# Shifting the SBUF places of three weight slots and two activation pools, with a smaller DMA scratch

## Chip, cores and metric

One core of a Trainium2 chip runs the whole program. The metric is the time of one execution in microseconds on the device, the median of several runs. [...]

## What is computed

Linear attention with an exponential feature map, then two gated feed-forward layers on the same 2304 tokens, all in float32.

```python
# q, k, v: (4, 8, 576, 64), w_phi: (64, 128)
def phi(x):
    proj = np.einsum('bhsd,df->bhsf', x, w_phi)
    proj = proj - np.max(np.abs(proj), axis=-1, keepdims=True)
    return np.concatenate([np.exp(proj), np.exp(-proj)], axis=-1)
q_p, k_p = phi(q), phi(k)
kv = np.einsum('bhsf,bhsd->bhfd', k_p, v)
z = np.sum(k_p, axis=2)
attn = np.einsum('bhsf,bhfd->bhsd', q_p, kv) / (np.einsum('bhsf,bhf->bhs', q_p, z)[..., None] + 1e-06)
x = attn.transpose(0, 2, 1, 3).reshape(2304, 512)
# layer 1, then layer 2 the same with sigmoid(x @ w_gate) in place of silu(x @ w_gate)
x = (silu(x @ w_gate) * (x @ w_val)) @ w_out       # 512 -> 1536 -> 512
```

## The kernel before

**Stages.** The program begins with the attention (about the first 150 us of the span): small float32 matmuls on lines 688, 724, 751 and 787, beside which VectorE, ScalarE and GpSimd turn the packed weights into float32 (lines 522 to 554). Then come the two layers, each in two passes `hh` over half of the hidden columns (`hh` 0 and 1 are the first layer, 2 and 3 the second). A pass goes over five token blocks (`BLOCKS`: four of 512 tokens, one of 256) in the order `ROUTE[hh]`, and for each block over three pieces `p` of its weights (`NPAIR`). One (hh, block, p) is a unit.

**A unit.** Every float32 operand is split into a high and a low part in the type fp32r (`plan_halves`, lines 573 and 579: ScalarE casts the high part, VectorE subtracts for the low one), and a product is three matmuls, high by high, high by low, low by high. In a full unit the gate and value products are done with seven block products instead of eight (`PROD`); `product` on line 1024 issues them, each matmul with a weight tile of 128 x 128 as the stationary operand and 256 columns of x as the moving one. Each of the seven block products is 12 matmuls, so a full unit has 84 of them; a unit of the 256-token block has four block products, 48 matmuls. They write the PSUM banks `a` and `b`; ScalarE and VectorE combine them (lines 1044, 1050), apply the gate (1062), multiply (1067) and split the result into `uh` and `ul`. The second product of the unit, `accumulate`, is issued inside the next unit: 24 matmuls of 512 columns for a full unit. In passes 0 and 1 (line 1099) the weights `o` are stationary and `u` moves; in passes 2 and 3 (line 1101) `u` is stationary and `o` moves.

**Order.** It is written out: `ORDER` gives for a full unit 24 matmuls of `product`, 12 of `accumulate` ("a", "b"), 48 of `product`, 9 of `accumulate` ("c", "d0"), 12 of `product`, 3 of `accumulate` ("d1"). A table of times sorts all calls once, and each engine's instructions stand in that order. All data DMAs are issued from SyncE's queue.

**Places in SBUF.** A weight slot is the pool `w0`, `w1` or `w2` with the tiles `w{p}h`, `w{p}l`, `o{p}h`, `o{p}l`; piece p always uses slot p. The pools `x0` and `x1` hold `xh` and `xl`; blocks alternate between them: x0 has the first, third and fifth block of passes 0 and 1 and the second and fourth of passes 2 and 3, x1 has the others. Pool `u` holds `c0`, `c1`, `uh`, `ul`. The pool `stage` holds the pieces that DMAs load and store. Pools are stacked from the left or the right end of each partition; w2 and x1 are opened when the attention's own pools have been closed (`swap`). A weight slice of one matmul is 128 floats, 512 bytes in a partition; a slice of x is 1024 bytes and one of u or o as a moving operand 2048. So all slices of a tile begin at the same place modulo 512 as the tile itself.

Of the kernel before, what the change touches and what calls it, by code (L numbers as in the profile page):

```python
# [10 lines left out]
F32 = mybir.dt.float32  # L11
# [9 lines left out]
P = 128  # L21
# [12 lines left out]
LINE = 32  # L34
# [419 lines left out]
def body(ctx: ExitStack, tc: tile.TileContext, qT, kT, v, w_phi2, wpk, out):  # L454
    nc = tc.nc
# [7 lines left out]
            for k, side in enumerate(("left", "right"))]  # L463
    wides = [x.__enter__() for x in wide]
    pools = {w: ctx.enter_context(tc.tile_pool(name=w, bufs=1)) for w in ("w0", "w1")}
    stage = ctx.enter_context(tc.tile_pool(name="stage", bufs=1))
    pools["x0"] = ctx.enter_context(tc.tile_pool(name="x0", bufs=1))
    pools["u"] = ctx.enter_context(tc.tile_pool(name="u", bufs=1))

    xT = [dram.tile([KC, P, S], F32, name=f"xT{b}") for b in range(B)]  # L470
# [731 lines left out]
    def pool(name, side="left"):  # L1202
        return tc.tile_pool(name=name, bufs=1, side=side, reuse_waits="tile")

    edge = ctx.enter_context(pool("edge", "right"))
    edge.tile([P, 3 * LINE // 4], F32, name="edge")
    aq, ap, ak, ae = pool("aq"), *(pool(name, "right") for name in ("ap", "ak", "ae"))
    aq_, *ap_ = (x.__enter__() for x in (aq, ap, ak, ae))
    T0, ready = plan_attention(*ap_, aq_, 0.0)
# [1 line left out]
    def swap(old, side, *names):  # L1211
        for x in reversed(old):
            x.__exit__(None, None, None)
        for name in names:
            pools[name] = ctx.enter_context(pool(name, side))

    for k in range(2):
        at(ready["w"][1 - k], part_banks, k)
    at(ready["e"], swap, (ap, ak, ae), "right", "w2")
    at(ready["nd"], swap, (aq,), "left", "x1")  # L1220

    T0 += TS
# [85 lines left out]
```

## Time and profile before

| | us |
|---|---|
| median of 3 runs | 993.05 (992.68 to 998.37) |
| the profiled execution, its own time | 996.62 |
| its span, first to last instruction | 994.5 |
| PE busy in the span | 980.9 (99%) |
| VectorE, ScalarE, GpSimd busy | 692.4, 527.2, 38.8 |

The span is 2.1 us shorter than the profiled execution's own time, and that execution lies 3.6 us above the median. PE busy counts matmuls whose ends are modelled, so 99% says that PE always has a matmul under way, not how fast they follow each other; that is read from the starts of successive matmuls.

### The profile page before, as it was taken

To read this page: it belongs to the slowest core of one execution; us is meant where nothing else is said; L and a number is where in the kernel's file an instruction comes from. 1 tells how busy PE (TensorE), PEld (TensorE's weight loads), DVE (VectorE), ACT (ScalarE), POOL (GpSimd) and SP (SyncE) were. 2 spreads that over 40 slices of the span, in tenths; PEclk is the share of its full clock that TensorE was granted. 3 is DMA by queue.
4 is the path that set the end of the run, shared out by engine and by line. 5 is a ranking of instruction groups with operands and counts; after the bars stand their busy time and mean duration, and the time that the engine had idled before them with its cause. 6 is when DMAs were issued, how large, how long until landed. Compare 5 with 4: busy or idle time off the path is not lost.

```text
span 994.5 us, 20911 instructions
## 1 busy us (share of the span) xinstructions
PE 980.9 (99%) x8632; PEld 891.5 (90%) x8632; DVE 692.4 (70%) x1220; ACT 527.2 (53%) x977; POOL 38.8 (4%) x40
## 2 busy tenths in 40 slices
PE   7999999999999999999999999999999999999998
PEld 6777778999999999999999999999999999999997
DVE  6999888938757795368787897486677834555343
ACT  5988977535545564264454574455546534334321
POOL 1433210000000000000000000000000000000000
PEclk9999999999999999999999999999999999999999
DMA  7566876436535532066554442446416002132011
GB/s 239 167 216 211 262 240 197 149 126 182 196 118 153 183 96 83 1 198 213 155 174 134 167 156 77 141 141 197 144 70 191 23 21 86 64 128 86 1 44 42
DMA packets 67551, 136.00 MB, mean 137 GB/s; under 512 B 9408, under 2 KB 35712, under 8 KB 67456
## 3 DMA queue, kind: packets, MB, share of 16 engines
q1 hardware_dynamic: 67456, 134.68, 42.4%
q8 instruction: 67, 1.10, 0.4%
q14 instruction: 28, 0.23, 0.1%
HBM read 94.66 MB, written 39.99 MB: 135 GB/s over the span
## 4 chain that ended last, share of the span: by engine, by line
PE 95%; DVE 3%; DMA 1%; ACT 0%; issue 0%; SPq 0%; DVEq 0%; ACTq 0%
PE a L1024 30%; PE b L1024 23%; PE c L1101 8%; PE c L1099 8%; PE d L1099 8%; PE d L1101 6%; PE d L787 5%; PE c L724 3%; PE w L688 3%; DVE sub L697 1%; DVE m L695 1%; PE w L751 1%; DMA xT<-nd 1%; DMA x<-kT 0%; ACT eq L771 0%
## 5 line engine op out<-in xcount | busy, mean ns | idle before, releaser
L1050 DVE TENSOR_TENSOR c<-b,c 128x512 f32<-128x512 f32 x96 | 66.0, 687 | 118.9 <-PE b L1024 109.9
L1062 ACT ACTIVATE c<-c 128x256 f32<-128x256 f32 x96 | 50.3, 525 | 147.0 <-DVE c L1050 147.0
L1044 ACT COPY c<-a 128x512 f32<-128x512 f32 x96 | 56.4, 587 | 111.9 <-PE a L1024 109.3
L573 DVE TENSOR_TENSOR ul<-c,uh 128x512 fp32r<-128x512 f32 (+1 forms) x120 | 75.8, 635 | 33.3 <-ACT uh L579 32.5
L579 ACT CAST uh<-c 128x512 fp32r<-128x512 f32 (+1 forms) x120 | 69.3, 580 | 41.6 <-DVE c L1067 33.3
L1024 PE MATMUL a<-xh,w0h 128*128 128x256 f32 x288 | 80.7, 280 | 0.0
L1024 PE MATMUL a<-xh,w1h 128*128 128x256 f32 x288 | 80.5, 280 | 0.0
L1024 PE MATMUL a<-xh,w2h 128*128 128x256 f32 x288 | 80.5, 279 | 0.0
L1024 PE MATMUL a<-xl,w0h 128*128 128x256 f32 x288 | 80.3, 279 | 0.0
L1024 PE MATMUL a<-xl,w2h 128*128 128x256 f32 x288 | 80.3, 279 | 0.0
L1024 PE MATMUL a<-xl,w1h 128*128 128x256 f32 x288 | 80.3, 279 | 0.0
L1024 PE MATMUL a<-xh,w0l 128*128 128x256 f32 x288 | 80.2, 279 | 0.0
L1024 PE MATMUL a<-xh,w2l 128*128 128x256 f32 x288 | 80.2, 279 | 0.0
L1024 PE MATMUL a<-xh,w1l 128*128 128x256 f32 x288 | 80.2, 278 | 0.0
L1067 DVE TENSOR_TENSOR c<-c 128x256 f32<-128x256 f32 (+1 forms) x96 | 52.9, 555 | 29.4 <-ACT c L1062 29.4
L1024 PE MATMUL b<-xh,w0h 128*128 128x256 f32 x224 | 62.5, 279 | 0.0
L1024 PE MATMUL b<-xh,w0l 128*128 128x256 f32 x224 | 62.4, 279 | 0.0
L1024 PE MATMUL b<-xh,w2l 128*128 128x256 f32 x224 | 62.4, 279 | 0.0
L1024 PE MATMUL b<-xh,w1l 128*128 128x256 f32 x224 | 62.4, 279 | 0.0
L1024 PE MATMUL b<-xl,w0h 128*128 128x256 f32 x224 | 62.4, 279 | 0.0
L1024 PE MATMUL b<-xh,w1h 128*128 128x256 f32 x224 | 62.4, 278 | 0.0
L1024 PE MATMUL b<-xl,w1h 128*128 128x256 f32 x224 | 62.4, 278 | 0.0
(183 smaller groups left out, 3028.5 us busy)
## 6 DMA issues: line engine op xcount, KB each, us to landing
raw<-wpk SPq DMA_DIRECT2D x72, 512.0 KB, 5.0
wf<-wcv SPq DMA_DIRECT2D x40, 256.0 KB, 2.8
a<-wf SPq DMA_DIRECT2D x20, 512.0 KB, 5.3
b<-xo SPq DMA_DIRECT2D x16, 512.0 KB, 6.1
part<-o SPq DMA_DIRECT2D x13, 512.0 KB, 6.2
o<-part SPq DMA_DIRECT2D x13, 512.0 KB, 4.7
wfo<-wcv SPq DMA_DIRECT2D x20, 256.0 KB, 4.9
v<-v SPq DMA_DIRECT2D x18, 264.0 KB, 7.3
```

Of the source, the lines that this page charges most:

```text
L573: nc.vector.tensor_tensor(out=lo, in0=src, in1=hi, op=ALU.subtract)
L579: nc.scalar.copy(hi, src)
L688: nc.tensor.matmul(r["ps"][:, i, n, c], r["x"][d, c, n * P:(n + 1) * P], w2[d], start=True, stop=True)
L724: nc.tensor.matmul(kv[qd, b][h // 2][u * 64:(u + 1) * 64, c * P:c * P + VW], e[r0:r1, h % 2, n, h // 2, s, u], r["v"][r0:r1, n, h], start= ...
L787: nc.tensor.matmul(pn[i * w:(i + 1) * w, :m], f, e[:, h, c, :m], start=(c == 0), stop=(c == 1))
L1024: nc.tensor.matmul(o, f[:, c], x[:, c], start=k == first and w == 0 and c == 0 and m == 0, stop=c == 1 and m == 2, skip_group_check=True)
L1044: nc.scalar.copy(part_of(r, d), parts(r, src))
L1050: nc.vector.tensor_tensor(out=c, in0=parts(r, "zy x"[d]), in1=c, op=ALU.add)
L1062: nc.scalar.activation(o, g, AF.Silu if hh < 2 else AF.Sigmoid)
L1067: nc.vector.tensor_tensor(out=o, in0=v, in1=places(r, j, 0, d)[1], op=ALU.mult)
L1099: nc.tensor.matmul(ps[:, :n], a[:, k], x, start=st, stop=sp)
L1101: nc.tensor.matmul(ps, x[:, k], a, start=st, stop=sp)
```

## The change

[...] No instruction, operand shape, wait or order is altered: on each engine the same instructions stand in the same order with the same waits, and only the addresses in SBUF differ. The tiles `gap1`, `gapx`, `gapx1` and `edge` are never written or read. (Lines are added too, so that what stands on line 1024 before stands on line 1026 after, 1099 on 1101, and 1101 on 1103.)

```diff
     pools = {w: ctx.enter_context(tc.tile_pool(name=w, bufs=1)) for w in ("w0", "w1")}
+    pools["w1"].tile([P, 96], F32, name="gap1")
     stage = ctx.enter_context(tc.tile_pool(name="stage", bufs=1))
     pools["x0"] = ctx.enter_context(tc.tile_pool(name="x0", bufs=1))
+    pools["x0"].tile([P, 32], F32, name="gapx")
     pools["u"] = ctx.enter_context(tc.tile_pool(name="u", bufs=1))
...
     edge = ctx.enter_context(pool("edge", "right"))
-    edge.tile([P, 3 * LINE // 4], F32, name="edge")
+    edge.tile([P, 136], F32, name="edge")
...
         for name in names:
             pools[name] = ctx.enter_context(pool(name, side))
+            if name == "x1":
+                pools[name].tile([P, 16], F32, name="gapx1")
...
-    nc = bacc.Bacc("TRN2", target_bir_lowering=False, num_devices=1)
+    nc = bacc.Bacc("TRN2", target_bir_lowering=False, num_devices=1, dynamic_dma_scratch_size=1024)
```

The addresses in the two built programs, in bytes modulo 512:

| tiles | before | after |
|---|---|---|
| w0 (w0h, w0l, o0h, o0l) | 128 | 128 |
| w1 | 128 | 0 |
| w2 | 384 | 448 |
| x0 (xh, xl) | 320 | 320 |
| x1 | 320 | 384 |
| u (uh, ul, c0, c1) | 320 | 320 |
| stage (loaded and stored pieces) | 128 | 0 |
| attention tiles on the right side (x, ek) | 384 | 448 |

The distance from the weights to x, address of x less that of the weights, modulo 512:

| | before | after |
|---|---|---|
| x0 with w0, w1, w2 | 192, 192, 448 | 192, 320, 384 |
| x1 with w0, w1, w2 | 192, 192, 448 | 256, 384, 448 |
| line 1099, u with o0, o1, o2 | 192, 192, 448 | 192, 320, 384 |
| line 1101, o0, o1, o2 with u | 320, 320, 64 | 320, 192, 128 |

## Rows read from the trace of the kernel before

**Rows 1.** The page: span, busy time by engine, PE's granted clock in 40 slices.
```profile
span 994.5 us, 20911 instructions
...
PE 980.9 (99%) x8632; PEld 891.5 (90%) x8632; DVE 692.4 (70%) x1220; ACT 527.2 (53%) x977; POOL 38.8 (4%) x40
...
PEclk9999999999999999999999999999999999999999
```

**Rows 2.** The page: share of the span by engine in the chain that ended last.
```profile
PE 95%; DVE 3%; DMA 1%; ACT 0%; issue 0%; SPq 0%; DVEq 0%; ACTq 0%
```

**Rows 3.** Waits of all engines and of PE: line waited for, us in total, times, longest.
```profile
DVE c L1050 <- PE b L1024: 109.9, 34, 6.9
ACT c L1044 <- PE a L1024: 109.3, 66, 3.6
...
PE w L688 <- DMA x<-kT: 4.6, 1, 4.6
PE w L688 <- DVE sub L697: 2.1, 2, 1.2
```

**Rows 4.** The page: DMA queues, packets, MB, share of 16 engines.
```profile
q1 hardware_dynamic: 67456, 134.68, 42.4%
q8 instruction: 67, 1.10, 0.4%
q14 instruction: 28, 0.23, 0.1%
```

**Rows 5.** Timeline of PE, pass 0: start us, us, line, tiles; 12 matmuls of 1099, then 48 of 1024.
```profile
200.14 0.39 PE L1099 MATMUL c<-uh,o2h 128*128 128x512 f32 x1
...
202.93 0.28 PE L1024 MATMUL a<-xh,w0h 128*128 128x256 f32 x1
...
208.58 0.39 PE L1099 MATMUL c<-uh,o2h 128*128 128x512 f32 x1
```

**Rows 6.** The same timeline, going on: 9 matmuls of 1099 after 208.58, then 12 of 1024.
```profile
210.68 0.28 PE L1024 MATMUL a<-xh,w0h 128*128 128x256 f32 x1
...
212.04 0.39 PE L1099 MATMUL d<-uh,o2h 128*128 128x512 f32 x1
```

**Rows 7.** Timeline of PE, pass 1: 24 matmuls of 1024 with slot w2.
```profile
392.86 0.28 PE L1024 MATMUL a<-xh,w2h 128*128 128x256 f32 x1
...
395.69 0.39 PE L1099 MATMUL c<-uh,o1h 128*128 128x512 f32 x1
```

**Rows 8.** Timeline of PE, pass 2: 12 matmuls of 1101, then 48 of 1024 (5, then 43).
```profile
621.11 0.39 PE L1101 MATMUL c<-o2h,uh 128*128 128x512 f32 x1
...
623.86 0.28 PE L1024 MATMUL a<-xh,w0h 128*128 128x256 f32 x1
...
624.45 0.28 PE L1024 MATMUL a<-xh,w0l 128*128 128x256 f32 x1
...
629.32 0.39 PE L1101 MATMUL c<-o2h,uh 128*128 128x512 f32 x1
```

**Rows 9.** Tile w2h, stretch 160 to 553 us: ns min/median/max of one, first and last start.
```profile
L1024 PE MATMUL b<-xh,w2h x100: 281/281/281, 183.3 to 521.8; 128*128 128x256 f32 x100
```

**Rows 10.** The same for the stretch 600 to 950 us.
```profile
L1024 PE MATMUL b<-xh,w2h x100: 276/276/276, 604.7 to 935.0; 128*128 128x256 f32 x100
```

**Rows 11.** The page: DMA issues, KB each, median us from issue to landing.
```profile
raw<-wpk SPq DMA_DIRECT2D x72, 512.0 KB, 5.0
```

## The prediction

> **What bounds the kernel now.** I read the page first. PE has a matmul under way for 980.9 of 994.5 us, at a granted clock of full speed in every slice [rows 1], and it makes up 95% of the chain that ended last [rows 2]. So other engines count only where PE waits for them. The list of waits says that they don't: VectorE and ScalarE wait for PE, 109.9 and 109.3 us on their main lines, while PE's own longest waits are one of 4.6 us for the first load of k and 2.1 us for VectorE, both in the attention [rows 3]. What is left to change is how fast PE's matmuls follow each other, and the page's busy time doesn't show that. The timeline does, by the starts of successive matmuls.
>
> In pass 0, 48 matmuls of line 1024 start between 202.93 and 208.58 us: 5.65 us over 48 is 117.7 ns each. The 12 of line 1099 ahead of them take 202.93 less 200.14, 2.79 us, 233 ns each [rows 5]. In pass 2, after 5 matmuls in 0.59 us (118 ns each), 43 of line 1024 start between 624.45 and 629.32: 113.3 ns each; the 12 of line 1101 ahead of them take 2.75 us, 229 ns each [rows 8]. [...] In pass 0 a run of 12 follows 9 matmuls of line 1099 and takes 1.36 us, 113.3 ns each [rows 6], while the run of 48 that follows 12 of them has 117.7 from end to end [rows 5]. The modelled duration of a matmul splits in the same way: slot w2's matmuls into bank b, which stand only in the long runs, are all 281 ns in the first two passes and all 276 ns later [rows 9, 10]. So in passes 0 and 1 a full unit runs mostly at the slow pace, and in passes 2 and 3 mostly at the fast one.
>
> **The change part by part.** The profiled execution took 996.62 us for a span of 994.5; the terms below are changes to that, and the median of the runs shown, 993.05, lies 3.57 us lower, so I carry their sum to 993.05.
>
> *The smaller scratch.* [...] All 67456 data packets go through the hardware queue q1, and the other two queues carry 95 packets of instructions [rows 4]; no GpSimd queue appears. I take 0, with nothing in the rows for a gain or a loss.
>
> *New addresses for DMAs.* The loaded pieces of `stage` go from 128 to 0 modulo 512. A 512 KB load lands 5.0 us after issue [rows 11], and PE waited for a DMA once, 4.6 us [rows 3]. A gain can be no more than those 4.6 us; a loss of a tenth on one load is 0.5 us in front of that one wait. The later loads are hidden behind PE's own work. If that cover went, each late load would cost what it is late, but they are issued ahead of use and no PE wait on them shows. I take 0.
>
> *New addresses for VectorE, ScalarE and GpSimd.* Their operations wait for PE for 100 us and more on single lines [rows 3], and that slack hides a few nanoseconds on an instruction. Only the attention has waits of PE on VectorE, 2.1 us in all, which bounds a gain; a loss of 1% on work there would be hundredths of those waits. I take 0.
>
> *New addresses for PE.* Here is the whole question: do the distances between the stationary and the moving slices set the pace? No row shows the new distances, so I bound it from both sides with the paces seen. A full unit in passes 0 and 1 is 72 matmuls at 117.7, 12 at 113.3 and 24 at 233 ns: 8.47 + 1.36 + 5.59 = 15.43 us. In passes 2 and 3 it is three entries of 5 at 118, 69 at 113.3 and 24 at 229: 1.77 + 7.82 + 5.50 = 15.09 us. There are 24 full units of each kind (four blocks, three pieces, two passes), and 6 units of the small block with 48 products each, for which I add 0.2 us each wherever the pace turns. From below: everything at 113.3, and 226.6 (twice that, an estimate) for 512 columns, is 9.52 + 5.44 = 14.96 us a unit; that saves 0.47 x 24 + 0.13 x 24 + about 1.6 = 16 us. From above: everything at 117.7 and 233 is 15.48 us, which costs 0.39 x 24 + 0.05 x 24 + about 1.5 = 12 us.
>
> Between -16 and +12 us I take 0, for two reasons. First, before the change slot w2 already stands 256 bytes from w0 and w1 modulo 512, and it makes no difference: 24 matmuls with w2 in pass 1 take 2.83 us, 117.9 ns each [rows 7], as w0 has 117.7, and w2 turns fast in passes 2 and 3 as w0 does [rows 8, 10]. Second, the pace changes within a pass and between passes while every address stays as it is [rows 5, 6, 8], so what has run just before decides it, not the place. Against this stands that line 1099 has 233 ns and line 1101 has 229, and what was swapped there is which operand moves, and with it the distance, 192 or 448 against 320 or 64. So places may count. But then the new table of distances mixes known and unknown values over the same units (w0 with x0 keeps 192; others get 320, 384, 256), and part of the gain in one half is lost in the other.
>
> [...]
>
> **The rivals.** *The places decide, and passes 0 and 1 get the fast pace.* For it: two stable paces exist, so a shift of phase could move a run from one to the other, and 72 of 84 products in these passes are slow [rows 5, 9]. Against it: w2's own shift did nothing [rows 7]. If every full unit there takes the 15.09 us of the later passes, that is 0.34 x 24 + 1.2 = 9.4 us, so 983.6 us; with line 1099 down to 226.6 ns and the entries gone too it goes to 977.
>
> *The places decide, and passes 2 and 3 fall into the slow pace.* There 69 of 84 products in a full unit run fast [rows 8, 10] under distances of 192 and 448, and four of the six distances between x and weights are new. If a run after line 1101 stays at 118 ns instead of turning fast after 5 matmuls, each full unit costs 0.34 us more, and this comes to +9.4 us with the small block, 1002.4 us; with the few stretches at 113.3 ns of passes 0 and 1 lost as well it is 1005. It decides from the point where more than half of these runs no longer turn.
>
> *The change does not do what it says.* It does shift the addresses; but if only the place modulo 256 or 128 counts, many distances are equal again (modulo 128, x0 with w0 and w1 stays at 64), and at most two thirds of the products can change. That gives at most two thirds of either rival, 6 us, and lies within my forecast's band.
>
> **How the numbers follow.** Forecast, no change of the pace, or changes that cancel to under 1%: 0.50, 993.0 us, and its own range is 989 to 997. Fast first half: 0.28, 983.6 us and below. Slow second half: 0.20, 1002.4 us and above. A transfer or the scratch after all: 0.02. One per cent, about what a measurement of this kernel can tell from no change, is 9.9 us: faster begins at 983.1, slower at 1003. Of the fast rival I put 6 in 10 below its border, 0.17; of the slow one a little over 6 in 10 above its border, 0.13; the rest, 0.70, is within 1%. The range of 980 to 1005 reaches into both rivals, up to the slow one's end, and leaves out the last 3 us of the fast one, which need every run to turn.
>
> **What would show it right or wrong.** Right: line 1026 in the changed kernel again has 281 ns for w2h into b up to 553 us and 276 ns from 600 us, runs of 48 in passes 0 and 1 at 117.7 ns a start and in passes 2 and 3 at 113.3 after 5 matmuls at 118, lines 1101 and 1103 at 233 and 229 ns. Wrong: x0 and x1 blocks, or the three slots, get different paces in the same pass, which would show that the distance counts; or a third pace appears, under 113 or over 118 ns, which none of my bounds holds. A new PE wait on a DMA in the passes would prove my second zero wrong.

## The result and the profile after

The changed kernel, with four empty places between pools and 1,024 bytes of DMA scratch, takes 1008.47 us, the median of 4 runs (1007.22 to 1009.72); the kernel before took 992.87 us beside it (4 runs, 989.73 to 998.37). The ratio is 1.014, with a 95% interval of 1.0106 to 1.0174: the change makes the kernel slower. I had forecast 993.0, and the top of my range was 1005. (In the batches of the experiments below the kernel before has medians of 996.1 to 997.2 us, so its four runs here may lie on the quick side; against those medians 1008.47 us is 1.1 to 1.2% more.)

The profiled execution has a span of 1005.4 us, 10.9 more than before. The page, against [rows 1]: PE's busy time grew by 12.1 us, the granted clock stayed at 1.00, nobody else has more to do (VectorE 692.4 before, ScalarE 527.2).

```profile
span 1005.4 us, 20911 instructions
...
PE 993.0 (99%) x8632; PEld 902.2 (90%) x8632; DVE 693.5 (69%) x1220; ACT 527.4 (52%) x977; POOL 38.8 (4%) x40
...
PEclk9999999999999999999999999999999999999999
```

The list of waits, against [rows 3] (lines are 2 higher), shows no new wait of PE: the longest is still the first load of k, and the wait for VectorE is shorter.

```profile
DVE c L1052 <- PE b L1026: 115.2, 36, 7.0
ACT c L1046 <- PE a L1026: 113.5, 68, 3.6
...
PE w L690 <- DMA x<-kT: 4.4, 1, 4.4
PE w L690 <- DVE sub L699: 1.4, 2, 1.2
```

So the time went where the busy share doesn't show it, into the spacing of the matmuls. The timeline of PE (start us, modelled us, line, tiles), for the unit of [rows 5] in pass 0, block in x1, slot w0:

```profile
200.61 0.40 PE L1101 MATMUL c<-uh,o2h 128*128 128x512 f32 x1
...
203.39 0.28 PE L1026 MATMUL a<-xh,w0h 128*128 128x256 f32 x1
...
209.14 0.40 PE L1101 MATMUL c<-uh,o2h 128*128 128x512 f32 x1
```

The 48 products take 5.75 us, 119.8 ns each. They had 117.7. The same view in pass 2, first with slot w2 and the block in x1, then with slot w0 and the block in x0, the unit of [rows 8]:

```profile
610.04 0.28 PE L1026 MATMUL a<-xh,w2h 128*128 128x256 f32 x1
...
615.48 0.39 PE L1103 MATMUL c<-o1h,uh 128*128 128x512 f32 x1
...
622.41 0.39 PE L1103 MATMUL c<-o2h,uh 128*128 128x512 f32 x1
...
625.18 0.28 PE L1026 MATMUL a<-xh,w0h 128*128 128x256 f32 x1
...
630.84 0.39 PE L1103 MATMUL c<-o2h,uh 128*128 128x512 f32 x1
```

The run with w2 still has the best pace, 5.44 us over 48, 113.3 ns. The run with w0 has 5.66 us, 117.9 ns, where [rows 8] had 118 for five and 113.3 for the rest. The two runs stand 15 us apart, in one pass. In before, slot w2 had one modelled duration for all its matmuls of xh into b in a stretch [rows 9, 10]; now it has several in both stretches (tile w2h; ns min/median/max):

```profile
L1026 PE MATMUL b<-xh,w2h x100: 276/281/285, 183.7 to 522.5; 128*128 128x256 f32 x100
```
```profile
L1026 PE MATMUL b<-xh,w2h x100: 276/281/285, 605.9 to 944.6; 128*128 128x256 f32 x100
```

What separates the first unit, at 119.8 ns, from these two is the place of its operands: their distance is 256, where the two runs of pass 2 have 448 and 192. Those two have the same distance modulo 256, so what separates them from each other is something else; `w2_only` below shows a cause. For every matmul I took the distance of the moving slice from the stationary one modulo 512 bytes (from the addresses in the program) and its time from its start to that of the next matmul (from the records of the trace), and averaged over all products of a kind, 336 or 432 each, in ns:

| moving, stationary | before: distance | passes 0, 1 | passes 2, 3 | after: distance | passes 0, 1 | passes 2, 3 |
|---|---|---|---|---|---|---|
| x0, w0 | 192 | 117.6 | 114.1 | 192 | 116.9 | 117.0 |
| x0, w1 | 192 | 117.7 | 114.3 | 320 | 117.0 | 117.6 |
| x0, w2 | 448 | 117.3 | 114.3 | 384 | 118.6 | 119.6 |
| x1, w0 | 192 | 117.5 | 115.0 | 256 | 119.7 | 119.6 |
| x1, w1 | 192 | 117.2 | 114.5 | 384 | 119.0 | 118.8 |
| x1, w2 | 448 | 117.2 | 114.3 | 448 | 116.8 | 116.3 |

Where the distance became a multiple of 128, 118.6 to 119.7 ns; where it stayed 64 off such a multiple, 116.3 to 117.6. The sums of all starts: products of passes 0 and 1 from 270.6 to 271.8 us, products of passes 2 and 3 from 263.6 to 272.2, the output matmuls (those of `accumulate`) from 151.4 to 150.8 and from 148.6 to 150.3. That is +1.2, +8.6, -0.6 and +1.7, in sum +10.9, the whole growth of the span. Half of the 4608 products (2304) now stand at a multiple of 128. At before's means (270.6 and 263.6 us over 2304 each, 117.45 and 114.41 ns) they would take 7.6 us less than they do; the other half lost 2.2 us at distances whose remainder did not change.

### The profile page after: what moved, and what is told of

Read it like the earlier page. It is cut to its first block, busy times and chain, and to the rows that moved or that the text cites. A ratio compares the mean times of both kernels' runs of the same rounds, so it can differ in the third digit from the quotient of the medians.

```text
span 1005.4 us, 20911 instructions
## 1 busy us (share of the span) xinstructions
PE 993.0 (99%) x8632; PEld 902.2 (90%) x8632; DVE 693.5 (69%) x1220; ACT 527.4 (52%) x977; POOL 38.8 (4%) x40
## 4 chain that ended last, share of the span: by engine, by line
PE 96%; DVE 2%; ACT 1%; issue 0%; DMA 0%; SPq 0%; ACTq 0%; DVEq 0%
PE a L1026 30%; PE b L1026 24%; PE c L1103 8%; PE c L1101 7%; PE d L1101 7%; PE d L1103 6%; PE d L789 5%; PE w L690 4%; PE c L726 3%; PE w L753 1%; DVE sub L699 1%; DVE m L697 0%; DMA x<-kT 0%; ACT eq L773 0%; ACT ek L706 0%
## 5 line engine op out<-in xcount | busy, mean ns | idle before, releaser
L1046 ACT COPY c<-a 128x512 f32<-128x512 f32 x96 | 56.2, 586 | 115.6 <-PE a L1026 113.5
L1026 PE MATMUL b<-xh,w2h 128*128 128x256 f32 x224 | 63.0, 281 | 0.0
L1026 PE MATMUL b<-xl,w2h 128*128 128x256 f32 x224 | 62.8, 281 | 0.0
```

What stands on the lines that cost most here:

```text
L1026: nc.tensor.matmul(o, f[:, c], x[:, c], start=k == first and w == 0 and c == 0 and m == 0, stop=c == 1 and m == 2, skip_group_check=True)
L1046: nc.scalar.copy(part_of(r, d), parts(r, src))
```

## The experiments

My theory was now that the distance modulo 128 decides. The rivals were the absolute place, the smaller scratch, and a pace that depends on something else in the run. All kernels below are the kernel before with a scratch of 1,024 bytes and the edit shown. Each ratio is to runs of before on the same chip, whose medians were 996.1 to 997.2 us.

**The scratch alone.**

```diff
-    nc = bacc.Bacc("TRN2", target_bir_lowering=False, num_devices=1)
+    nc = bacc.Bacc("TRN2", target_bir_lowering=False, num_devices=1, dynamic_dma_scratch_size=1024)
```

> The kernel before with the DMA scratch cut to 1,024 bytes and nothing else: every SBUF address moves by 15,360 bytes, a multiple of 512, so every place modulo 512 stays. Theory A (the distance between the stationary and the moving slices, x less w modulo 128, sets the pace: 64 gives 113.3 or 117.8 ns, 0 gives 118.5 to 120 ns): no change, 993 us, ratio 1.000 within 0.3%. Rival S (the scratch or the high address bits cost the time): 1004 us or more, with matmuls of x0 with w0 in passes 2 and 3 at 117 ns instead of 114.

Measured 996.55 us, ratio 0.9988 (0.9966 to 1.0009). Neither the scratch nor an address that is lower by 15,360 bytes, a multiple of 512, costs anything that these runs can tell. Its profile held something else. The timeline of PE shows the run of 48 with w0 in pass 0 (5.65 us, 117.7 ns each) and in pass 1 (5.44 us, 113.3), at the same addresses:

```profile
203.48 0.28 PE L1024 MATMUL a<-xh,w0h 128*128 128x256 f32 x1
...
209.13 0.39 PE L1099 MATMUL c<-uh,o2h 128*128 128x512 f32 x1
...
368.18 0.28 PE L1024 MATMUL a<-xh,w0h 128*128 128x256 f32 x1
...
373.62 0.39 PE L1099 MATMUL c<-uh,o2h 128*128 128x512 f32 x1
```

In this execution all runs of 48 of pass 1 had 113.3 ns, in the profile of before none had. The products of passes 0 and 1 took 267.0 us instead of 270.6. So the pace of these passes differed between two executions with the same places modulo 512; a like difference between executions of one program, which no two profiles here show, could account for some of before's spread from 989.7 to 998.4 us.

**All places moved, distances kept.**

```diff
+        if w == "w0":
+            pools[w].tile([P, 16], F32, name="gap0")
...
-    edge.tile([P, 3 * LINE // 4], F32, name="edge")
+    edge.tile([P, 136], F32, name="edge")
```

> Weight slots, x pools and u all moved by 64 bytes modulo 512, so that every distance is as before (192 and 448) and x stands at 0 modulo 128, the slots at 64. Theory A (only the distance counts): paces and time of before, 993 us within 0.4%, 117.8 ns in the long runs of passes 0 and 1 and 113.3 in those of 2 and 3. Rival P (the place itself counts, x at 0 modulo 128 or weights at 64 modulo 128): 119 to 120 ns in all products, 1006 us or more.

Measured 997.02 us, ratio 1.0005 (0.9987 to 1.0022). The products take 270.8 us in passes 0 and 1 and 263.6 in passes 2 and 3, where before had 270.6 and 263.6, and the unit of [rows 8] has its 48 products in 5.46 us, 113.8 ns each:

```profile
625.02 0.28 PE L1028 MATMUL a<-xh,w0h 128*128 128x256 f32 x1
...
630.48 0.39 PE L1105 MATMUL c<-o2h,uh 128*128 128x512 f32 x1
```

The absolute place does not count, as far as a common shift of 64 bytes can tell. That the distance does, the next run shows.

**All distances a multiple of 128.** (u and x1 move with x0. The distances become 256, 256 and 0, so all are multiples of 256 too.)

```diff
     pools["x0"] = ctx.enter_context(tc.tile_pool(name="x0", bufs=1))
+    pools["x0"].tile([P, 16], F32, name="gapx")
```

> The kernel before with pools x0, u and x1 moved by 64 bytes: every distance is 0 modulo 128 (256, 256 and 0 with w0, w1, w2), places of the three slots and the two x pools as equal or unequal as before. Theory A: all 4608 products at 118.5 to 120 ns against 115.9 on average before, +12 to +19 us, and the time 1006 to 1012 us; no run at 113.3 ns in any pass. Rival D (only unlike places cost): 993 us with the paces of before.

Measured 1014.77 us, ratio 1.0185 (1.0165 to 1.0206). The timeline of the unit of [rows 5]: 48 products in 5.75 us, 119.8 ns each.

```profile
203.40 0.28 PE L1025 MATMUL a<-xh,w0h 128*128 128x256 f32 x1
...
209.15 0.40 PE L1100 MATMUL c<-uh,o2h 128*128 128x512 f32 x1
```

The products average 120.0 ns in passes 0 and 1 and 119.7 in passes 2 and 3 (276.5 and 275.8 us), whether they follow 3, 9 or 12 other matmuls. At these distances there is one pace for 256 columns, and it is the slowest mean of all these runs. The 512-column matmuls are not hurt (230 to 231 ns).

**All distances 64 off such a multiple, but different ones.** Slots w0, w1, w2 at 128, 0 and 256, x0 and x1 at 320 and 448.

```diff
+    pools["w1"].tile([P, 96], F32, name="gap1")
...
+    pools["x0"].tile([P, 32], F32, name="gapx")
...
+                pools[name].tile([P, 32], F32, name="gapx1")
...
+    edge.tile([P, 56], F32, name="edge")
```

> All five pools at places of their own modulo 512 (w 128, 0, 256; x 320, 448), as in the changed kernel, but with every distance at 64 modulo 128 (x0: 192, 320, 64; x1: 320, 448, 192). Theory A: no run settles at 118.5 to 120 ns; only 113.3 and 117.8 appear, and the time lies between 980 and 1001 us, by how many runs get which. Rival D (five different places as such cost, because runs no longer follow a fitting one): as slow as the changed kernel, 1005 to 1010 us, with means of 119 ns in some groups of x and w.

Measured 1001.75 us, ratio 1.0056 (1.0038 to 1.0075), just above what I expected. No run behind the attention has 119 ns or more, as the theory asks; rival D, with 1005 us and means of 119 ns, falls. But passes 2 and 3 lost much of their 113.3 ns all the same: their products take 268.8 us instead of 263.6. So a distance of 64 modulo 128 allows the best pace and does not secure it.

**One pool of the change at a time.** First only x1, so that its three distances become 0 or 256:

```diff
+            if name == "x1":
+                pools[name].tile([P, 16], F32, name="gapx1")
```

> One part of the change alone: pool x1 moved by 64 bytes (distances of x1 256, 256 and 0, all others as before; scratch 1,024). Theory A (a distance of 0 modulo 128 has no pace of 113.3 ns and settles near 120): the 1008 products with x1 in passes 0 and 1 go from 117.3 to about 119.7 ns (+2.4 us), the 1296 in passes 2 and 3 from 114.6 to about 119.7 (+6.6 us), those with x0 stay: +9 us, ratio 1.009. Rival B (the loss is in the change of distances from run to run, not in the distance of the run itself): products with x0 in passes 2 and 3 lose the 113.3 ns too, since blocks alternate, and the loss is 12 us or more; or, with no loss in either, 0.

Measured 1004.23 us, ratio 1.0081 (1.0062 to 1.0099). In pass 2 the timeline has a run of 48 from x1 and one from x0, with the same slot w0:

```profile
578.64 0.28 PE L1024 MATMUL a<-xh,w0h 128*128 128x256 f32 x1
...
584.39 0.40 PE L1099 MATMUL c<-uh,o2h 128*128 128x512 f32 x1
...
625.25 0.28 PE L1024 MATMUL a<-xh,w0h 128*128 128x256 f32 x1
...
630.72 0.39 PE L1101 MATMUL c<-o2h,uh 128*128 128x512 f32 x1
```

x1 has 5.75 us, 119.8 ns; x0 has 5.47 us, 114.0, as in before. (The run from x1 is the first unit of the pass and still follows line 1099; in before it took 5.66 us, 117.9 ns. The later x1 runs, behind line 1101, go from 113.8 or 113.9 to 120.0 ns.) Then only slot w2, by 64 bytes:

```diff
-    edge.tile([P, 3 * LINE // 4], F32, name="edge")
+    edge.tile([P, 136], F32, name="edge")
```

> Another part alone: slot w2 moved by 64 bytes (distances of w2 128 for both x pools, of o2 with u 128; all others as before; scratch 1,024). Theory A: the 768 products with w2 in passes 2 and 3 go from 114.3 to about 119 ns (+3.6 us), the 768 in passes 0 and 1 from 117.3 to about 119 (+1.3 us), line 1101 with o2 from 231 to 234 ns (+0.6 us): +5.5 us, ratio 1.0055. Rival B (what ran just before counts): besides this, the products with w0 in passes 2 and 3, whose runs come after the matmuls with o2, no longer turn to 113.3 ns and stay at 117.8, +2.7 us more, ratio 1.008, while those with w1, which come after o0, keep 114 ns.

Measured 1001.83 us, ratio 1.0051 (1.0034 to 1.0068). The timeline of pass 2 shows slot w2, and the next unit's w0, whose own distance is unchanged:

```profile
606.43 0.28 PE L1024 MATMUL a<-xh,w2h 128*128 128x256 f32 x1
...
612.13 0.40 PE L1101 MATMUL c<-o1h,uh 128*128 128x512 f32 x1
...
621.85 0.28 PE L1024 MATMUL a<-xh,w0h 128*128 128x256 f32 x1
...
627.50 0.39 PE L1101 MATMUL c<-o2h,uh 128*128 128x512 f32 x1
```

w2 takes 5.70 us, 118.8 ns each. The run with w0 behind it takes 5.65 us, 117.7, where before had 113.3 after five. What is new ahead of that run is o2: it lies in slot w2 and moved with it. So a run's pace also hangs on the output matmuls ahead of it, as the rival had said. Its 2.7 us for that came to only 0.8 in the sums of starts, since the runs of 24 with w0 kept the best pace, and the products of passes 0 and 1 took 1.5 us less than in before. The two parts, 1.0081 and 1.0051, add up to 1.0132 and the change has 1.014, but that they agree is in part luck: the products of x1 with w2 are at a multiple of 128 in each part and not in the change (448), and the parts leave out the move of w1.

**Which of the two paces at 64 modulo 128?** First I shifted all x and u by 128, which exchanges the distances modulo 256 of passes 0 and 1 with those of passes 2 and 3, and then only those of passes 0 and 1.

```diff
+    pools["x0"].tile([P, 32], F32, name="gapx")
```

> Pools x0, x1 and u moved by 128 bytes: all distances of x stay at 64 modulo 128, but 320 and 64 (64 modulo 256) take the place of 192 and 448; line 1099 gets 64 and line 1101 192 modulo 256, the other way round than before. Theory A with modulo 128 alone: paces by pass as before, 993 to 997 us, ratio within 0.3% of 1. Theory A2 (modulo 256 counts for the runs of 512 columns, and these set the pace of the products after them): line 1099 falls from 233 to about 230 ns and line 1101 rises from 229 to about 233; the runs of 48 in passes 0 and 1 turn to 113.3 ns and the products of passes 2 and 3 to 117.7: the halves change places, the sum stays within 0.4%.

Measured 1003.6 us, ratio 1.0073 (1.0048 to 1.0098). Theory A with modulo 128 alone fails, and of theory A2 only half held. The output matmuls changed places as it says (means by slot: line 1099 from 232.6 to 234.5 ns down to 230.3 to 232.0, line 1101 from 229.0 to 230.9 up to 233.3 to 234.9). Passes 2 and 3 lost the best pace wholly (the run of 48 with w0, below: 5.65 us, 117.7 ns), but passes 0 and 1 did not get it: 117.8 to 117.9 ns in every run after the program's first.

```profile
625.26 0.28 PE L1025 MATMUL a<-xh,w0h 128*128 128x256 f32 x1
...
630.91 0.39 PE L1102 MATMUL c<-o2h,uh 128*128 128x512 f32 x1
```

```diff
+                off = 32 if hh < 2 else 0
+                xs[hh, j] = [pools[f"x{k}"].tile([P, 14 * NQ + 128], R32, tag=x, name=x)
+                             [:, off:off + 14 * NQ].rearrange("p (c q n) -> p c q n", c=2, q=7)
...
+            off = 32 if hh < 2 else 0
+            r["u", f] = [pools["u"].tile([P, 2 * NQ + 128], R32, tag=f"u{x}{f}", name=f"u{x}{f}")
```

> x and u begin 128 bytes later within their tiles in passes 0 and 1 and where they were in passes 2 and 3 (tiles 512 bytes longer, scratch 1,024), so line 1099 has 64 modulo 256 with products at 64, and line 1101 keeps 64 with products at 192. Theory A2: the runs of 48 and 12 in passes 0 and 1 take 113.3 ns instead of 117.8 and 113.8, those of 24 stay at 117.7; line 1099 takes about 230 ns: per full unit 48 x 4.4 + 24 x 3 = 0.28 us, 24 units 6.8 us, ratio 0.993, passes 2 and 3 unchanged. Rival (modulo 128 alone): ratio 1.000 within 0.3%.

Measured 996.69 us, ratio 0.9993 (0.9981 to 1.0005); the expectation failed. The place modulo 256 is not enough to choose the pace. In the profile, the products of the second half of pass 0 go at 113.3 ns, whether they follow 12, 9 or 3 output matmuls; in pass 1, at the same places, they go at 117.8 behind all three (but for its first run):

```profile
304.52 0.28 PE L1026 MATMUL a<-xh,w2h 128*128 128x256 f32 x1
...
309.96 0.39 PE L1102 MATMUL c<-uh,o1h 128*128 128x512 f32 x1
...
312.02 0.28 PE L1026 MATMUL a<-xh,w2h 128*128 128x256 f32 x1
...
313.38 0.39 PE L1102 MATMUL d<-uh,o1h 128*128 128x512 f32 x1
...
396.01 0.28 PE L1026 MATMUL a<-xh,w2h 128*128 128x256 f32 x1
...
401.67 0.40 PE L1102 MATMUL c<-uh,o1h 128*128 128x512 f32 x1
...
403.74 0.28 PE L1026 MATMUL a<-xh,w2h 128*128 128x256 f32 x1
...
405.15 0.40 PE L1102 MATMUL d<-uh,o1h 128*128 128x512 f32 x1
```

The runs of 48 and 12 take 5.44 and 1.36 us in pass 0 and 5.66 and 1.41 us in pass 1.

**Is it the order of the three output matmuls?** In line 1101 the first two of three share the moving operand, in line 1099 the stationary one. `mirror` gives line 1099 the order of the other; `mirror_u` also shifts u by 128 bytes in passes 0 and 1, so that its distance to o is 64 modulo 256, as on line 1101.

```diff
+            three = ((wh, uh), (wl, uh), (wh, ul)) if hh < 2 else ((wh, uh), (wh, ul), (wl, uh))
+            for m, (a, x) in enumerate(three):
```

> The kernel before (scratch 1,024, all places modulo 512 as before), but on line 1099 the three matmuls of a product come as high by high, low weights by high u, high weights by low u, so that the moving operand stays for two matmuls in a row, as it does on line 1101. Theory C (besides the distance, the run of 512 columns just before sets which of the two paces a run of products falls into, and line 1101 always hands over so that they turn to 113.3 ns because of its order of operands): the products of passes 0 and 1 turn to 113.3 ns after up to 5 matmuls, 114.3 on average against 115.6 to 117.3, a gain of 3 to 7 us, ratio 0.993 to 0.997; line 1099 keeps about 233 ns. Rival: the order of operands does nothing, ratio 1.000 within 0.3%.

> The same order of operands, and u 128 bytes later within its tiles in passes 0 and 1, so that line 1099 has the distance of line 1101, 64 modulo 256, and x keeps 192 and 448. Theory C: passes 0 and 1 run as 2 and 3 do: line 1099 at 229 ns instead of 233 (384 matmuls counted in full units, -2.4 us) and products at 114.3 ns; ratio 0.990 to 0.995, the fastest of all. Rival: line 1099 falls to 229 ns but the products stay at 117.8, ratio 0.998.

`mirror`: 993.08 us, ratio 0.9971 (0.9952 to 0.999). But in its profile every pace of the products stays (270.6 us in passes 0 and 1, as in before), so the order alone does not turn them. What the 0.3% are stays open: the profiled execution, 996.29 us, is one of the slowest of the 12, and no profile shows a quick one. `mirror_u`: 997.64 us, ratio 1.0024 (1.0007 to 1.004), outside both expectations. Its products in passes 0 and 1 are at 117.5 to 117.8 ns in every run once the attention is over, also the runs of 12 behind 9, which have 113.3 in before [rows 6]; here 48 take 5.65 us and 12 take 1.41:

```profile
189.13 0.28 PE L1024 MATMUL a<-xh,w2h 128*128 128x256 f32 x1
...
194.78 0.40 PE L1101 MATMUL c<-uh,o1h 128*128 128x512 f32 x1
...
196.86 0.28 PE L1024 MATMUL a<-xh,w2h 128*128 128x256 f32 x1
...
198.27 0.40 PE L1101 MATMUL d<-uh,o1h 128*128 128x512 f32 x1
```

The theory that the order brings the best pace falls, and the distance of the output matmuls does not bring it either.

**Other remainders**, one execution each: x0, u and x1 shifted by 32 bytes (the edit below) and by 96 (24 floats), which gives 96 and 32 modulo 128.

```diff
+    pools["x0"].tile([P, 8], F32, name="gapx")
```

> Pools x0, x1 and u moved by 32 bytes: distances of x are 224 and 480, 96 modulo 128 (scratch 1,024). Theory A knows only 0 and 64 modulo 128; by it a place between lies between: products at 113 to 120 ns, the time between 993 and 1015 us. Rival (only steps of 64 bytes count, 96 acts as 64): paces and time of before.

> Pools x0, x1 and u moved by 96 bytes: distances of x are 288 and 32, 32 modulo 128 (scratch 1,024). Theory A: products at 113 to 120 ns, the time between 993 and 1015 us. Rival (only steps of 64 bytes count, 32 acts as 0): 120 ns in all products, 1010 to 1015 us.

Measured 1010.99 and 1006.24 us, with no interval. The products have 118.2 to 118.6 ns at a remainder of 96, and 116.7 to 117.4 at 32, in all passes. Both rivals fall: 96 does not act as 64, and 32 does not act as 0. A remainder of 64 has two steady paces, 113.3 and 117.8. A remainder of 0 is not one case: multiples of 256 have 120.0 (`even_all`), while the distances 128 and 384 have means of 118.6 to 118.8 (slot w2 in `w2_only`) and up to 119.9 in runs of the changed kernel.

**The hand-over.** Passes 2 and 3 of before have three things, of which `mirror_u` gave passes 0 and 1 only the first two: products at 192, output matmuls at 64, and at the hand-over a multiple of 256 from the last operand that moved in an output matmul to the weights that the first product loads. `mirror_places` gives passes 0 and 1 all three.

```diff
+            off = 48 if hh < 2 else 0
+            return [pool.tile([P, 2 * DM + 128], R32, tag=f"o{p}{x}", name=f"o{p}{x}{hh}")
+                    [:, off:off + 2 * DM].rearrange("p (c n) -> p c n", c=2) for x in "hl"]
...
+            off = 16 if hh < 2 else 0
+            r["u", f] = [pools["u"].tile([P, 2 * NQ + 128], R32, tag=f"u{x}{f}", name=f"u{x}{f}")
+                         [:, off:off + n] for x in "hl"]
```

> In passes 0 and 1 only, u stands 64 bytes and the output weights 192 bytes further inside their tiles, so that these passes have the places of passes 2 and 3 with the roles swapped: o to u 64 modulo 128, x to w still 192, and from the last output weights to the first x 128 modulo 256 instead of 64. Theory 'the hand-over sets the pace': a run of products that follows an output matmul whose places are a multiple of 128 bytes off turns to 113.3 ns as it does in passes 2 and 3, and the output matmuls take 229 instead of 233 ns; then 9 us go, ratio 0.991. Rival 'only the number of output matmuls before a run counts, odd turns it and even keeps it': the products of these passes stay at 117.7 and 113.3 ns as they are, and the ratio is 0.997 to 1.000.

(The text on record has 128 modulo 256 from the last output weights to the first x; the addresses give 0. The intended places, those of passes 2 and 3, are the ones that ran.) Measured 988.7 us (988.14 to 989.58), ratio 0.9919 (0.9905 to 0.9934): the version that beats both kernels. The unit of [rows 5] again: 12 output matmuls in 2.75 us (229 ns), then 48 products in 5.47 us, 114.0 ns.

```profile
199.79 0.39 PE L1103 MATMUL c<-uh,o2h 128*128 128x512 f32 x1
...
202.54 0.28 PE L1027 MATMUL a<-xh,w0h 128*128 128x256 f32 x1
...
208.01 0.39 PE L1103 MATMUL c<-uh,o2h 128*128 128x512 f32 x1
```

The products of passes 0 and 1 take 264.8 us, where the profile of before had 270.6, and the output matmuls 149.9, from 151.4. Against `mirror_u`, which had the products' and the output matmuls' distances modulo 256, the place at the hand-over is what was added (and the order of `mirror` left out, which had changed no pace). The hand-over back, from products to output matmuls, moved with it. The hand-over alone is not enough: passes 2 and 3 of `x_by_128` have the same multiple of 256 there and stay at 117.8 ns, with products at 64 and output matmuls at 192 modulo 256.

**The number of output matmuls ahead of a run.** In before, a run of passes 0 and 1 is at 113.3 ns behind 9 and at 117.7 behind 12 [rows 5, 6]. This kernel moves three of the 12 behind the run of 48; no place changes.

```diff
+ORDER_FIRST = (1, 5, "a", "b0", 6, 3, 7, 2, "b1", "c", "d0", 4, "d1")
...
+                ORDER_FIRST if full and hh < 2 else ORDER[full]:
```

> No place changes. In passes 0 and 1 three of the twelve output matmuls ahead of the run of 48 products stand three output matmuls later, so the groups are of 9, 12 and 3 instead of 12, 9 and 3. Theory 'an odd number of output matmuls turns the pace, an even one keeps it': the run of 48 follows 9 and goes at 113.3 ns instead of 117.8, the run of 12 follows 12 and stays at 113.3, the run of 24 follows 3 and stays at 117.8; that is 48 x 4.45 ns in 24 units, 5.1 us less, ratio 0.995. Rival 'the group ahead has nothing to do with it, only the kind of product has': the runs of 48 stay at 117.8 ns, the ratio is 1.000 or, for one more change between the two shapes, 1.001.

Measured 993.8 us (992.23 to 994.38), ratio 0.9968 (0.9955 to 0.998), between the two expectations. The run of 48 in pass 0 and in pass 1:

```profile
202.79 0.28 PE L1027 MATMUL a<-xh,w0h 128*128 128x256 f32 x1
...
208.45 0.39 PE L1102 MATMUL d<-uh,o2h 128*128 128x512 f32 x1
...
498.08 0.28 PE L1027 MATMUL a<-xh,w1h 128*128 128x256 f32 x1
...
503.53 0.39 PE L1102 MATMUL d<-uh,o0h 128*128 128x512 f32 x1
```

5.66 us (117.9 ns) in pass 0, 5.45 us (113.5) in pass 1. Pass 1 goes as expected: 24 at 117.8, 9 output matmuls, 48 at 113.3, 12 output matmuls, 12 at 113.3, 3 output matmuls, 24 at 117.8. Pass 0 is its negative: 24 at 113.3, then 48 and 12 at 117.8. But for one or two runs in each pass, both obey one rule, that an odd number turns the pace and an even one keeps it; I had only reckoned with one starting point. With 12 full units a pass, that is 48 x 4.45 ns x 12 = 2.6 us from pass 1 and (24 - 12) x 4.45 ns x 12 = 0.6 us from pass 0, 3.2 us against the profile of before; the sums of starts have 267.2 us instead of 270.6, 3.4 less. (That 0.0032 of 996.57 us is 3.2 too is in part luck, since the pace of a pass can differ between executions, as in pass 1 of before and of `scratch_only`, 117.7 and 113.3 ns in the runs of 48.) The rival, that the group ahead has no part in it, falls. But the rule belongs to these places, with line 1099 at 192 modulo 256: where line 1099 stands at 64, groups of 9 and 3 turn nothing, in `by_layer` (113.3 ns behind all groups in the second half of pass 0, 117.8 in pass 1) and in `mirror_u` (117.5 to 117.8).

## Why the prediction was wrong

*The smaller scratch, 0*: right. With the scratch alone cut, `scratch_only` has a ratio of 0.9988, its interval around 1; what uses the scratch no run shows.

*New addresses for DMAs, and for VectorE, ScalarE and GpSimd, 0*: right. PE's one wait for a DMA is 4.4 us instead of 4.6, and that for VectorE 1.4 instead of 2.1.

*New addresses for PE, "I take 0"*: this step failed. The question was the right one, and the place had an effect of 10.9 us in the trace. Both reasons for the zero were true rows read too far.

- "Slot w2 already stands 256 bytes from w0 and w1 modulo 512, and it makes no difference." It doesn't, because the paces repeat: 192 and 448 are the same modulo 128 and modulo 256 (117.6 and 117.3 ns for x0 with w0 and w2 in passes 0 and 1, 114.1 and 114.3 in passes 2 and 3). A row for an effect of distance that shows only two distances a period apart can't bound the effect. I had named this ("if only the place modulo 256 or 128 counts") and drew from it only that fewer products would change and that 6 us would bound it. Half of them did change, but 256 and 384 were a new class, for which no row had a pace, and these products alone cost 7.6 us.
- "The pace changes within a pass and between passes while every address stays as it is." True, and it still does (113.3 and 117.7 ns in `scratch_only`). But that is a choice between the two paces of one class of distances, and the class is set by the place: in `even_all` the products have 119.7 to 120.0 ns in all passes.

*From above, 117.7 and 233 ns, +12 us*: the sum held the 10.9 us between the two profiles, but not for its reason. It supposed two paces, and the runs have a third, 120.0 ns at multiples of 256 and 118.6 or more at 128 and 384. With all products there, `even_all` cost 1.85%, 18 us, more than my bound. The median rose by 15.6 us, more than the spans did, since the profiled execution of before lay above its median (996.62 against 992.87) and that of the changed kernel below (1007.38 against 1008.47). I had written that "a third pace appears, under 113 or over 118 ns, which none of my bounds holds" would prove me wrong; it stands in the first unit shown above. The other sign, unlike paces of slots and x blocks in one pass, came as well.

*The rival "passes 2 and 3 fall into the slow pace"*: it came nearest. That half of the program holds 8.6 of the 9.8 us that the products lost. Its mechanism is in part the true one. The products at a multiple of 128 went past that pace, and account for 7.6 us; those that kept their remainder fell to 117.8 in many runs, as the rival says, for 2.8 us in passes 2 and 3 (0.6 came back in passes 0 and 1). Its 9.4 us lie only 1.5 below the 10.9 of the trace, in part by luck: the products of passes 2 and 3 now average 118.2 ns, a mix of 119.3 and 116.9 and not one pace of 117.8. The rest of the way from 1002.4 to 1008.47 us is how the medians lie to the profiled executions.

*The rival "passes 0 and 1 get the fast pace"* did not come with this change, but it is to be had: `mirror_places` gained 0.81%, 8 us, where the rival had 9.4.

*No wait, and yet three paces.* The list of PE's waits is empty from 150 us of the span on, in before as in the changed kernel, but the same 256-column matmul takes 113.3, 117.8 or 120.0 ns with nothing but places or the matmuls ahead altered. So the distance at which the two operands of a matmul lie is not without effect on its time. What in the chip makes it so no run shows.

Still open: why an odd number of output matmuls turns the pace at before's places, and why a remainder of 64 has two paces. And the hand-over was tried as a whole: which of the distances there (moving to next weights, last weights to next x, or those of the way back) carries it was not told apart.

## What to carry over

When a kernel is bound by back-to-back matmuls, read the time from start to start; the busy share was 99% in before and in the changed kernel, at spans of 994.5 and 1005.4 us. Look at the distance modulo 128 bytes between the slice that moves and the slice that is loaded as weights, and keep it away from 0 (here 0 gave means of 118.6 to 120.0 ns, and 64 gave the best, 113.3 ns or 117.8). Look at the hand-over between groups of matmuls too, where the opposite was best: in `mirror_places` (988.7 us, ratio 0.9919) the last moving slice and the next weights lie a multiple of 256 apart, with products at 192 and output matmuls at 64 modulo 256. And before an effect is bounded from rows, ask whether the rows hold more than one value of what is about to change.

## What the runs showed that I had not expected

- The mean pace of a 256-column matmul by the distance modulo 128: at 0, 120.0 ns (multiples of 256) or about 118.7 (128 and 384, in `w2_only`); 116.7 to 117.4 at 32 and 118.2 to 118.6 at 96, from one execution each; 113.3 or 117.8 at 64. The 512-column matmuls: 230 to 231 ns at 0 in `even_all`; in before, 229 to 231 at 64 and 233 to 235 at 192 modulo 256.
- Moving weights, x and u by 64 bytes together did nothing that shows (1.0005, 0.9987 to 1.0022).
- A pace is carried from one run of products to the next. At before's places in passes 0 and 1 an odd number of 512-column matmuls turned it between 113.3 and 117.8 ns and an even number kept it (in `split_b`, but for one or two runs in each pass); in `by_layer` neither turned it. In `scratch_only` the run of 48 with w0 has 117.7 ns in pass 0 and 113.3 in pass 1 at the same addresses, which fits with before's spread from 989.7 to 998.4 us. `mirror_places`, whose run of 48 behind 12 output matmuls has 114.0 ns and whose products of passes 0 and 1 take 264.8 us, has 988.1 to 989.6.
